# Causal attention with decay and a mixer: the 64-key tile transposed two query tiles at a time, its low part moved by DMA

## The chip, the cores and the metric

The kernel runs on one core of a Trainium2 chip. The metric is the device time of one execution in microseconds (us). PE is the matmul engine, DVE the vector engine, ACT the scalar engine, POOL is GpSimd, and SP issues the DMAs.

## The reference

For 8 batches and 8 heads, with 576 positions and head dimension 64, then a mixer over tokens and channels:

```python
scores = scale * np.matmul(q, k.transpose(0, 1, 3, 2))
cum = np.cumsum(np.log(np.clip(f, 0.0001, 1.0)), axis=-1)
decay = cum[:, :, :, None] - cum[:, :, None, :]
scores = np.where(causal, -1000000000.0, scores + decay)
attn = np.exp(scores - np.max(scores, axis=-1, keepdims=True))
attn = attn / (np.sum(attn, axis=-1, keepdims=True) + 1e-09)
x = np.matmul(attn, v)                    # heads side by side: 512 channels
h = np.maximum(x.T @ w_tok1, 0.0) @ w_tok2
u = x + h.T
out = u + np.maximum(u @ w_ch1, 0.0) @ w_ch2
```

## The kernel before, in words

The 576 positions are five tiles: tile 0 has 64, tiles 1 to 4 have 128. There are 64 heads, one after another, in an attention stage; the token mixer of each batch and part of the channel mixer run inside that stage, the rest of the channel mixer behind it (the channel stage). Numbers that need more than one pass of the fast matmul are split in a high part and a low part ("hi" and "lo"), and a product is made of three matmuls. The first four heads (`fv`) are done without parts.

For each head: PE makes the scores of each query tile against all earlier keys (L1031); DVE finds the minimum of the negated scores (L1038); ACT makes the exponentials into the tile `pr` (L1045), with the five query tiles side by side; DVE makes the reciprocals of the sums (L1063, L1066); POOL multiplies each query tile by them (L1073, five instructions). Then PE transposes `pr` block by block into PSUM (L1087): 15 blocks of query tile and key tile per head. For key tiles 1 to 4 ACT writes the high part to SBUF (L699) and DVE the low part (L708).

Key tile 0 has 64 keys, so its blocks give 64 rows. The block of query tile 0 is transposed in the group of key tile 2 (`t2`), the four others in the group `trs0`. Their high parts go to rows 0 to 63 of the tile `p0`, their low parts to the tile `low`, both in two pieces (64 and 512 columns). POOL then moves the low parts from `low` to rows 64 to 127 of `p0` (`hi_pool`, L702). One matmul over all 128 rows (L1159, L1160) then takes the high and low part at once. There is one buffer each of `p0` and `low`; L1159 is the first matmul of a head's output and reads `p0`, and the following head's `trs0` needs `p0` free.

The order on each engine is fixed before the launch: every operation gets a number for its place from the table `PR` (by kind of operation, `k0` to `k127`), and a planner goes through the engines in this order with its own costs and assigns buffers. Each engine, and SP as queue of the DMAs, works in this order and waits for what an instruction needs.

Of the kernel before, what the change touches and what calls it, by code (L numbers as in the profile page):

```python
# [15 lines left out]
P = 128  # L16
# [7 lines left out]
    k0=(0,),  # L24
    k1=(1, 0,),
# [17 lines left out]
    k20=(5, 16,),
    k21=(4, 10,),
    k22=(5, 10, 13, 19,),
    k23=(1, 0, 2, 4, 5, 3, 8, 6, 7, 21, 15, 18, 27, 25, 24, 36, 37, 35, 51, 53, 49, 56, 60, 52, 73, 75, 79, 91, 88, 87, 104, 105, 106, 114, 115, 116, 137, 135, 133, 145, 150, 147, 164, 167, 171, 179, 183, 185, 198, 202, 201, 213, 215, 217, 225, 230, 226, 240, 242, 241, 261, 263, 262, 275, 280, 279, 291, 293, 297, 308, 315, 310, 321, 327, 323, 343, 346, 341, 356, 357, 362, 373, 376, 375, 388, 394, 390, 405, 408, 406, 421, 425, 424, 437, 439, 438, 450, 452, 458, 464, 467, 472, 486, 491, 488, 503, 501, 500, 520, 523, 522, 534, 533, 536, 552, 554, 551, 564, 565, 568, 582, 589, 586, 601, 604, 606, 618, 621, 620, 633, 642, 637, 653, 656, 655, 673, 672, 669, 685, 690, 682, 699, 709, 703, 722, 718, 717, 735, 733, 737, 752, 754, 758, 763, 766, 769, 781, 787, 782, 796, 802, 801, 814, 816, 815, 832, 837, 834, 845, 863, 861, 857, 859, 872, 878, 891, 886, 894, 897, 906, 911, 923, 922, 929, 930, 937, 941, 946, 952, 955, 953, 959,),
    k24=(13, 10, 12, 14, 20, 29, 27, 31, 32, 33, 41, 30, 38, 34, 35, 56, 47, 49, 53, 55, 67, 61, 63, 60, 62, 76, 77, 79, 75, 78, 93, 95, 98, 92, 100, 101, 106, 108, 94, 97, 118, 119, 121, 123, 124, 139, 133, 137, 131, 134, 151, 153, 158, 152, 154, 160, 166, 168, 164, 167, 187, 186, 189, 183, 184, 195, 199, 202, 198, 200, 217, 219, 221, 224, 226, 232, 237, 238, 239, 241, 255, 257, 259, 256, 258, 267, 270, 272, 273, 275, 284, 288, 289, 285, 287, 299, 301, 303, 298, 300, 321, 323, 325, 322, 324, 333, 341, 343, 338, 340, 350, 352, 354, 359, 361, 370, 379, 380, 373, 376, 384, 391, 392, 385, 388, 405, 408, 409, 404, 406, 419, 421, 423, 427, 428, 438, 441, 443, 440, 442, 452, 460, 462, 456, 458, 476, 472, 474, 470, 473, 490, 492, 493, 491, 495, 505, 507, 509, 506, 508, 518, 520, 522, 526, 528, 543, 536, 538, 542, 544, 556, 561, 562, 558, 559, 576, 577, 579, 570, 573, 592, 594, 596, 593, 595, 608, 609, 611, 610, 614, 626, 631, 632, 627, 629, 645, 640, 643, 646, 649, 658, 667, 668, 662, 663, 675, 676, 678, 681, 683, 691, 694, 697, 693, 695, 709, 715, 717, 712, 714, 730, 732, 734, 733, 736, 752, 751, 753, 747, 749, 767, 771, 772, 760, 764, 781, 786, 787, 783, 784, 799, 794, 798, 793, 796, 811, 808, 809, 813, 814, 826, 827, 829, 831, 833, 837, 839, 842, 843, 845, 860, 861, 864, 856, 858, 870, 880, 881, 874, 878, 895, 889, 893, 888, 890, 904, 909, 911, 907, 908, 918, 932, 933, 929, 931, 934, 927, 928, 940, 945, 949, 960, 961, 955, 957, 962, 964, 967, 975, 976, 981, 990, 992, 987, 989, 994, 995, 997, 1006, 1007, 1017, 1016, 1021, 1020, 1022, 1028, 1024, 1025, 1031, 1034,),
# [610 lines left out]
def build(nc, env, dims):  # L658
# [296 lines left out]
    for n in range(HB):  # L955
# [139 lines left out]
        for g, kind, pb in (((3, 4), "t3", p34), ((2,), "t2", p2_), ((1,), "t1", p1_)):  # L1095
# [4 lines left out]
            def trs(ps=ps, blocks=blocks, w=w, first=g == (2,), tr=tr):  # L1100
# [965 lines left out]
```

## Time and profile before

| | us |
|---|---|
| median of 3 runs | 1017.48 (1015.66 to 1018.0) |
| the profiled execution | 1015.77 |
| its span | 1014.0 |
| PE busy in the span | 998.8 (99%) |
| DVE busy | 816.7 (81%) |
| ACT busy | 687.5 (68%) |
| POOL busy | 428.2 (42%) |

The span is the time from the first to the last instruction in the profile; the execution's own time lies 1.8 us above it. Matmuls are pipelined, so a PE that is busy all the time isn't a PE at its peak. POOL has next to nothing to do after the attention stage, so its share of the span says little about that stage.

### The profile page before, as it was taken

How to read it: one execution, taken by the hardware profiler on the slowest of the kernel's cores; microseconds unless marked ns; L12 is line 12 of the kernel's file. 1: busy time of each engine (PE TensorE's matmuls, PEld its weight loads, DVE VectorE, ACT ScalarE, POOL GpSimd, SP SyncE). 2: the span in 40 equal slices, each digit the busy share in tenths (PEclk: the TensorE clock that was granted, in tenths of full speed). 3: DMA queues.
4: the chain of work that ended last, by engine and by line, in shares of the span. 5: the costliest groups of instructions: out<-in, count | busy, mean ns of one | idle time of the engine just before them, and what ended most of it. 6: DMA issues, size and time to landing. Idle time of an engine off the chain costs nothing.

```text
span 1014.0 us, 19130 instructions
## 1 busy us (share of the span) xinstructions
PE 998.8 (99%) x6146; PEld 877.6 (87%) x6146; DVE 816.7 (81%) x1932; ACT 687.5 (68%) x1708; POOL 428.2 (42%) x530
## 2 busy tenths in 40 slices
PE   8999999999999999999999999999999999999998
PEld 5678899989999999999999988888888878888886
DVE  8899999898999897888885466879669756975695
ACT  7998899897888888878895533665266445543651
POOL 7688778878787886896862100000000000000000
PEclk9999999999999999999999999999999999999999
DMA  8865788876877765556426688727725762574054
GB/s 240 272 228 191 243 292 291 298 260 231 294 259 274 274 225 199 195 195 228 165 97 242 220 281 272 240 65 233 239 89 146 238 192 67 157 247 150 11 171 161
DMA packets 110595, 212.21 MB, mean 209 GB/s; under 512 B 13296, under 2 KB 51184, under 8 KB 109472
## 3 DMA queue, kind: packets, MB, share of 16 engines
q1 hardware_dynamic: 110496, 210.99, 62.4%
q8 instruction: 49, 0.80, 0.3%
q14 instruction: 50, 0.41, 0.1%
HBM read 113.26 MB, written 44.04 MB: 155 GB/s over the span
## 4 chain that ended last, share of the span: by engine, by line
PE 83%; DVE 8%; ACT 3%; issue 2%; DMA 2%; POOL 1%; SPq 0%; DVEq 0%; POOLq 0%; ACTq 0%
PE bank L1087 8%; PE bank L1576 6%; PE bank L1578 6%; PE bank L1577 6%; PE bank L1514 6%; PE bank L1516 6%; PE bank L1515 6%; PE bank L1031 5%; PE pair L1031 3%; PE pair L1169 3%; PE pair L1171 2%; ACT pr L1045 2%; PE bank L1686 2%; PE bank L1783 2%; PE bank L1687 2%
## 5 line engine op out<-in xcount | busy, mean ns | idle before, releaser
L1073 POOL TENSOR_SCALAR pr<-pr,rec 64x64 f32<-64x64 f32 (+4 forms) x320 | 171.6, 551 | 47.7 <-DVE rec L1066 18.2
L699 ACT ACTIVATE p<-bank 128x384 fp32r<-128x384 f32 (+3 forms) x300 | 130.4, 473 | 22.6 <-PE bank L1087 19.1
L1087 PE MATMUL bank<-ident,pr 128*128 128x128 f32 (+1 forms) x960 | 140.4, 274 | 4.7 <-DVE low L708 2.6
L1045 ACT ACTIVATE pr<-bank,nmin 64x64 f32<-64x64 f32 (+3 forms) x256 | 118.3, 471 | 12.5 <-DVE nmin L1038 10.4
L1087 PEld LDWEIGHTS bank<-ident,pr 128*128 128x128 f32 (+1 forms) x960 | 106.4, 131 | 21.6 <-DVE low L708 2.9
L708 DVE TENSOR_TENSOR p<-bank,p 128x384 fp32r<-128x384 f32 (+1 forms) x180 | 105.3, 590 | 10.6 <-ACT p L699 10.1
L1038 DVE CUSTOM_DVE_ANT_0 bank<-bank,mask 128x448 f32<-128x448 f32 (+3 forms) x256 | 106.5, 432 | 6.2 <-PE bank L1031 4.8
L1578 PE MATMUL bank<-ring,w2r 128*128 128x512 f32 x244 | 94.9, 389 | 0.0
L1031 PE MATMUL bank<-k 128*128 128x320 f32 (+1 forms) x480 | 83.3, 303 | 0.7 <-ACT pr L1045 0.6
L1576 PE MATMUL bank<-ring,w2r 128*128 128x512 f32 x212 | 82.5, 389 | 0.0
L1577 PE MATMUL bank<-ring,w2r 128*128 128x512 f32 x212 | 82.5, 389 | 0.0
L699 ACT ACTIVATE ring<-xt 128x512 fp32r<-128x512 f32 (+1 forms) x86 | 54.6, 649 | 35.8 <-DVE xt L1482 18.0
L1171 PE MATMUL pair<-p,vv 128*128 128x512 f32 x240 | 76.4, 321 | 0.0
L950 POOL TENSOR_TENSOR hl<-raw,hl 128x1152 fp32r<-128x1152 f32 x27 | 72.5, 2684 | 1.4
L1169 PE MATMUL pair<-p,vv 128*64 128x512 f32 x240 | 69.8, 332 | 0.0
L1031 PEld LDWEIGHTS bank<-k 128*128 128x128 f32 (+1 forms) x480 | 62.3, 176 | 3.3 <-ACT pr L1045 0.9
L699 ACT ACTIVATE ring<-h 128x512 fp32r<-128x512 f32 x63 | 38.3, 626 | 38.5 <-DVE h L1541 16.9
L708 DVE TENSOR_TENSOR low<-bank,p 64x512 fp32r<-64x512 f32 (+1 forms) x120 | 52.3, 442 | 10.8 <-ACT p L699 9.0
L699 ACT ACTIVATE ring<-bank 128x288 fp32r<-128x288 f32 (+2 forms) x96 | 47.1, 498 | 19.4 <-PE bank L1757 11.3
L702 POOL TENSOR_SCALAR p<-low 64x576 fp32r<-64x576 f32 x60 | 40.5, 676 | 40.2 <-DVE low L708 27.8
L705 POOL TENSOR_TENSOR ring<-xt,ring 128x576 fp32r<-128x576 f32 x32 | 45.9, 1442 | 25.4 <-ACT ring L699 25.1
L1045 ACT ACTIVATE pr<-pair,nmin 128x576 f32<-128x576 f32 x64 | 47.3, 739 | 10.2 <-DVE nmin L1038 7.1
(197 smaller groups left out, 3069.4 us busy)
## 6 DMA issues: line engine op xcount, KB each, us to landing
k<-hl SPq DMA_DIRECT2D x180, 288.0 KB
w2r<-sd SPq DMA_DIRECT2D x80, 256.0 KB
raw<-in_qk SPq DMA_DIRECT2D x60, 288.0 KB
w2r<-wd SPq DMA_DIRECT2D x60, 256.0 KB
vr<-in_v SPq DMA_DIRECT2D x32, 320.0 KB
ud<-xt SPq DMA_DIRECT2D x8, 1152.0 KB
pd<-part SPq DMA_DIRECT2D x32, 288.0 KB
dd<-in_w_ch SPq DMA_DIRECT2D x12, 512.0 KB
```

The source lines that it names most:

```text
L699: nc.scalar.activation(out, in_, func, scale=scale)
L708: nc.vector.tensor_tensor(out, in_, asf(hi), op=ALU.subtract)
L1031: nc.tensor.matmul(ps[:m, of : of + w], k[:, 0, i0 : i0 + m], k[:, 1, j0 : j0 + w], start=(x == 0), stop=(fq or x == 1))
L1038: nc.vector.tensor_tensor_reduce(x, x, E["mask"][:m, a : a + w], -1.0 / D**0.5, 3e38, op0=ALU.add, op1=ALU.min, accum_out=E["nmin"][sm][:m ...
L1045: nc.scalar.activation(at(pr)[:m, poff[t] : poff[t] + w], at(buf)[:m, of : of + w], AF.Exp, bias=E["nmin"][sm][:m, t : t + 1], scale=-1.0, ...
L1073: nc.gpsimd.tensor_scalar(x, x, r, 0.0, op0=ALU.mult, op1=ALU.add)
L1087: nc.tensor.transpose(out, at(pr)[:, poff[i] + start[j] : poff[i] + end[j]], E["ident"])
L1169: nc.tensor.matmul(x[:D], at(vv)[:, v0 + j, :D], at(pb)[:, 1, c0 : c0 + w], start=False, stop=last)
L1171: nc.tensor.matmul(x, at(vv)[:, v0 + j, :], at(pb)[:, 0, c0 : c0 + w], start=False, stop=last)
L1576: nc.tensor.matmul(o_, wh[:, ms], h_, start=first and pr == 0, stop=False, skip_group_check=not first)
L1577: nc.tensor.matmul(o_, wl[:, ms], h_, start=False, stop=False, skip_group_check=not first)
L1578: nc.tensor.matmul(o_, wh[:, ms], l_, start=False, stop=pr == PH - 1, skip_group_check=not first)
```

## The change

The five blocks of key tile 0 are no longer transposed one by one. Query tile 0 is transposed as a 64 x 64 block. Query tiles 1 and 3, and 2 and 4, go in pairs: POOL's normalisation writes the first 64 columns of query tile 1 to a place right ahead of query tile 3 (and those of 2 ahead of 4), for which `pr` has 64 columns more in two places, and one transpose of 128 columns turns both. The result has query tiles 1 and 2 in rows 0 to 63 and 3 and 4 in rows 64 to 127. So ACT writes high parts over all 128 rows in pieces of 320 and 256 columns, and DVE makes one low part of 128 x 320. Where the high part stands in rows 0 to 63 of `p0`, the low part is put in rows 64 to 127, and the other way round; two DMAs on SP move them there. The move by POOL is gone. Every number of the table `PR` is new. `hold`, a new field of the planner, and the costs changed with it bear on the planner's times alone.

```diff
-    poff = [sum(end[:t]) for t in range(NS)]
+    poff = [sum(end[:t]) + T0 * max(0, t - 2) for t in range(NS)]
+    MID = T0 + 2 * P
...
-        def norm(t, sm=sm, pr=pr):
...
+        def norm(t, a, z, to, sm=sm, pr=pr):
             m = size[t]
+            x, y = (at(pr)[:m, c : c + z - a] for c in (poff[t] + a, to))
+            nc.gpsimd.tensor_scalar(y, x, E["rec"][sm][:m, t // 2, t % 2 : t % 2 + 1], 0.0, op0=ALU.mult, op1=ALU.add)
...
         for t in (4, 3, 2, 1, 0):
+            a = T0 if t in (1, 2) else 0
+            p.op("POOL", d_pts(end[t] - a, 1), n + o["nrm"], lambda t=t, a=a, f=norm: f(t, a, end[t], poff[t] + a), rd=[("rec", sm)], wr=[(pr, t)], bufs=[pr])
+            if a:
+                p.op("POOL", d_pts(a, 1) + 50, n + o["nrm"], lambda t=t, a=a, f=norm: f(t, 0, a, poff[t + 2] - a), rd=[("rec", sm), (pr, t, "e")], wr=[(pr, t, "z")], bufs=[pr])
...
-                if first:
-                    tr(at(ps)[:T0, w : w + P], 0, 0)
...
-        def trs0(ps=ps, tr=tr):
-            for i in range(1, NS):
-                tr(at(ps)[:T0, (i - 1) * P : i * P], i, 0)
...
+        def trs0(ps=ps, pr=pr):
+            x, y = at(ps), at(pr)
+            nc.tensor.transpose(x[:, :T0], y[:T0, :P], E["ident"][:T0, :T0])
+            for z in (0, 1):
+                nc.tensor.transpose(x[:, T0 + z * P : T0 + (z + 1) * P], y[:, poff[z + 3] - T0 : poff[z + 3] + T0], E["ident"])
...
-            p.op("ACT", d_act(512), n + LAG + o["t0"] + o["hl"], lambda ps=ps, pb=p0_: hi_act(at(pb)[:T0, T0:], at(ps)[:T0, :]), rd=[ps], wr=[(p0_, "h1")], bufs=[ps, p0_])
+            p.op("ACT", d_act(MID), e0, lambda ps=ps, pb=p0_: hi_act(at(pb)[:, :MID], at(ps)[:, :MID]), rd=[ps], wr=[(p0_, 0)], bufs=[ps, p0_])
             p.op(
-                "DVE", d_dve(512), n + LAG + o["t0"] + o["hl"], lambda ps=ps, pb=p0_, lb=low: lo_dve(at(lb)[:, T0:], at(ps)[:T0, :], at(pb)[:T0, T0:]),
...
+                "DVE", d_dve(MID), e0, lambda ps=ps, pb=p0_, lb=low: lo_dve(at(lb), at(ps)[:, :MID], at(pb)[:, :MID]),
...
-            p.op(
-                "POOL", d_pts(S) + 110, n + LAG + o["t0"] + o["lo0"], lambda pb=p0_, lb=low: hi_pool(at(pb)[T0:, :], asf(at(lb))),
...
+            p.op("ACT", d_act(S - MID), e0, lambda ps=ps, pb=p0_: hi_act(at(pb)[:, MID:], at(ps)[:, T0:MID]), rd=[ps], wr=[(p0_, 1)], bufs=[ps, p0_])
+            dma(e0, lambda pb=p0_, lb=low: nc.sync.dma_start(asf(at(pb)[T0:, :MID]), asf(at(lb)[:T0])), 81920, dur=600, rd=[low], wr=[(p0_, 0)], bufs=[p0_, low])
+            dma(e0, lambda pb=p0_, lb=low: nc.sync.dma_start(asf(at(pb)[:T0, MID:]), asf(at(lb)[T0:, T0:])), 65536, dur=600, rd=[low], wr=[(p0_, 1)], bufs=[p0_, low])
...
-        ("pr", [P, 64 + 192 + 320 + 448 + 576], F32),
+        ("pr", [P, 64 + 192 + 320 + 64 + 448 + 64 + 576], F32),
...
-        ("low", [D, S], F32R),
+        ("low", [P, 64 + 256], F32R),
```

How the order moves is shown at two places. The numbers behind a name tell one buffer from another.

On PE in the middle of the attention stage, before the change: the transposes of one head (out of `pr_182`; the group of key tile 2 first, its fourth block is that of query tile 0; then key tile 1; then the four blocks of `trs0`), among output matmuls of the head ahead of it.

```order
L1087 MATMUL bank_65<-ident,pr_182 128x128 x3
L1087 MATMUL bank_65<-ident,pr_182 64x128
L1169 MATMUL pair_71<-p_189,vv_180 64x512
L1171 MATMUL pair_71<-p_189,vv_180 128x512
L1087 MATMUL bank_66<-ident,pr_182 128x128 x4
L1087 MATMUL bank_64<-ident,pr_182 64x128 x4
L1169 MATMUL pair_71<-p_188,vv_180 64x384
L1171 MATMUL pair_71<-p_188,vv_180 128x384
```

The same place with the change (line numbers are those of the changed kernel: L1119 and L1121 are `trs0`, L1088 the other blocks, L1156 and L1158 output matmuls, L1640 the mixer's transposes).

```order
L1119 MATMUL bank_64<-ident,pr_183 128x64
L1121 MATMUL bank_64<-ident,pr_183 128x128 x2
L1156 MATMUL pair_71<-p_189,vv_180 64x512
L1158 MATMUL pair_71<-p_189,vv_180 128x512
L1088 MATMUL bank_66<-ident,pr_183 128x128 x3
L1640 MATMUL bank_65<-ident,xt_151 128x128 x4
L1156 MATMUL pair_71<-p_187,vv_180 64x384
L1158 MATMUL pair_71<-p_187,vv_180 128x384
L1088 MATMUL bank_64<-ident,pr_183 128x128 x4
```

The tile's three transposes now stand ahead of the head's other groups, not behind them. From the row L1121 to the first matmul that reads this head's `p0` (L1146) follow 30 rows, with 15 transposes of 128 columns and matmuls of 7488 columns together.

On SP in the second half of the attention stage, before the change: k are the loads for the scores, raw those of q and k, dd, gd and ge weights on their way, ud the mixer's result.

```order
L964 DMA raw_172<-in_qk 64x1152
L1004 DMA k_176<-hl_175 64x1152
L1004 DMA k_178<-hl_175 64x2x576
L1004 DMA k_177<-hl_175 64x1152
L1004 DMA k_176<-hl_175 64x2x576
L1004 DMA k_177<-hl_175 64x2x576
L1004 DMA k_179<-hl_175 64x2x576
```

With the change, at the same place:

```order
L1137 DMA p_190<-low_191 64x256
L1136 DMA p_190<-low_191 64x320
L1722 DMA ud_130<-xt_150 128x2304
L910 DMA gd_116<-dd 128x1024
L1001 DMA k_178<-cc_192 2x1x576
L1007 DMA k_176<-hl_175 64x1152
L1137 DMA p_190<-low_191 64x256
L1136 DMA p_190<-low_191 64x320
L790 DMA dd<-in_w_ch 128x256
L967 DMA raw_172<-in_qk 64x1152 x2
L1007 DMA k_176<-hl_175 64x2x576
```

The two DMAs of each head's low part (L1136, L1137) stand between the loads, as pairs, and the loads of later heads stand behind them.

## Rows read from the trace of the kernel before

**Rows 1.** The page: busy time, share of the span and instructions of each engine.

```profile
PE 998.8 (99%) x6146; PEld 877.6 (87%) x6146; DVE 816.7 (81%) x1932; ACT 687.5 (68%) x1708; POOL 428.2 (42%) x530
```

**Rows 2.** Busy time by stretches: window, length, engines' busy us, clock, DMA share, GB/s.

```profile
60.00:541.00 481.00, 474.10 (x3662) 449.92 (x3661) 427.24 (x1225) 412.30 (x1139) 380.56 (x458) 1.00 0.66 232
541.00:1014.00 473.00, 467.58 (x2171) 390.96 (x2169) 338.38 (x548) 224.29 (x424) 5.75 (x4) 1.00 0.57 180
700.00:800.00 100.00, 100.00 (x443) 82.77 (x441) 78.12 (x119) 50.09 (x90) 0.00 (x0) 1.00 0.60 184
...
```

**Rows 3.** The chain that ended last: shares of the span by engine, by line.

```profile
PE 83%; DVE 8%; ACT 3%; issue 2%; DMA 2%; POOL 1%; SPq 0%; DVEq 0%; POOLq 0%; ACTq 0%
...
by line: PE bank L1087 8.1%; PE bank L1576 6.0%; PE bank L1578 6.0%; PE bank L1577 6.0%; PE bank L1514 6.0%; PE bank L1516 6.0%; PE bank L1515 5.9%; PE bank L1031 5.3%; PE pair L1031 2.6%; PE pair L1169 2.5%; PE pair L1171 2.5%; issue 2.3%;
```

**Rows 4.** Timeline of one head, 345 to 351 us: start, duration, instruction.

```profile
344.98 0.60 PE L1087 MATMUL bank<-ident,pr 128*64 128x128 f32 x4
...
345.68 0.60 ACT L699 ACTIVATE p<-bank 64x512 fp32r<-64x512 f32 x1
...
346.38 0.68 DVE L708 TENSOR_TENSOR low<-bank,p 64x512 fp32r<-64x512 f32 x1
...
347.88 0.19 DVE L708 TENSOR_TENSOR low<-bank,p 64x64 fp32r<-64x64 f32 x1
...
348.65 0.67 POOL L702 TENSOR_SCALAR p<-low 64x576 fp32r<-64x576 f32 x1
...
348.89 0.49 PE L1087 MATMUL bank<-ident,pr 128*128 128x128 f32 x3
...
351.07 0.39 PE L1159 MATMUL pair<-p,vv 128*128 128x512 f32 x1
```

**Rows 5.** Groups by line, whole span: count, busy us, mean ns, idle before.

```profile
L1087 PE MATMUL bank<-ident,pr 128*128 128x128 f32 (+1 forms) x960 | 140.4, 274 | 4.7 <-DVE low L708 2.6 <-DVE xt L1724 1.4 <-DVE rec L1066 0.2
```

**Rows 6.** Groups by line and shape, DVE, ACT and POOL, 60 to 541 us.

```profile
L708 DVE TENSOR_TENSOR low<-bank,p 64x512 fp32r<-64x512 f32 x59 | 39.9, 676 | 7.0 <-ACT p L699 6.2 <-issue 0.3
L708 DVE TENSOR_TENSOR low<-bank,p 64x64 fp32r<-64x64 f32 x59 | 12.2, 207 | 3.8 <-ACT p L699 2.8 <-issue 0.6
...
L699 ACT ACTIVATE p<-bank 64x512 fp32r<-64x512 f32 x59 | 34.7, 589 | 2.9 <-PE bank L1087 2.3
L699 ACT ACTIVATE p<-bank 64x64 fp32r<-64x64 f32 x59 | 12.5, 212 | 2.4 <-PE bank L1087 2.2
...
L702 POOL TENSOR_SCALAR p<-low 64x576 fp32r<-64x576 f32 x59 | 39.9, 676 | 40.1 <-DVE low L708 27.8 <-PE pair L1171 3.4 <-ACT xt L1209 2.5
L1073 POOL TENSOR_SCALAR pr<-pr,rec 128x320 f32<-128x320 f32 x58 | 31.0, 536 | 5.1 <-ACT p L699 4.4
L1073 POOL TENSOR_SCALAR pr<-pr,rec 128x192 f32<-128x192 f32 x58 | 25.3, 437 | 6.4 <-DVE rec L1066 2.8 <-ACT p L699 2.6 <-PE bank L1087 0.5
L1073 POOL TENSOR_SCALAR pr<-pr,rec 64x64 f32<-64x64 f32 x57 | 19.1, 337 | 7.0 <-PE pair L1031 3.5 <-ACT xt L1209 1.6 <-DVE rec L1066 1.1
```

**Rows 7.** DMA issues on SP, lines L998 and L1004: min/median/max ns.

```profile
L998 SPq DMA_DIRECT2D k<-cc x120: 557/632/1397, 26.6 to 515.8; - x120
...
L1004 SPq DMA_DIRECT2D k<-hl x180: 465/624/1516, 16.3 to 514.6; - x180
```

**Rows 8.** DMA issues in 60 to 541 us: transfer, count, KB each.

```profile
k<-hl SPq DMA_DIRECT2D x163, 288.0 KB
...
dd<-gd SPq DMA_DIRECT2D x4, 256.0 KB
```

**Rows 9.** Timeline, two DMAs and the instructions that waited for them.

```profile
465.48 0.54 SPq L964 DMA_DIRECT2D raw<-in_qk  x1
...
468.90 1.16 POOL L942 TENSOR_SCALAR hl<-raw 128x1152 fp32r<-128x1152 f32 x1 [0.57 <-DMA raw<-in_qk]
...
497.05 0.54 SPq L973 DMA_DIRECT2D vr<-in_v  x1
...
501.40 0.74 ACT L940 ACTIVATE vv<-vr 128x640 fp32r<-128x640 f32 x1 [0.72 <-DMA vr<-in_v]
```

More of the change, by code (lines that the diff above doesn't have):

```diff
@@ L23 @@
 PR = dict(
-    k0=(0,),
-    k1=(1, 0,),
+    k0=(1,),
+    k1=(0, 1,),
     k2=(0,),
@@ L498 @@
 class Op:
-    __slots__ = ("eng", "dur", "head", "tail", "lat", "fn", "prio", "bufs", "need", "outs", "ready", "start", "idx", "port", "grp")
+    __slots__ = ("eng", "dur", "head", "tail", "lat", "fn", "prio", "bufs", "need", "outs", "ready", "start", "idx", "port", "grp", "hold")
 class Plan:
@@ L528, in op @@
         o.head = o.tail = 0.0
+        o.hold = hold
         if eng == "PE":
@@ L561, in run @@
         engine_at = dict.fromkeys(queue, 0.0)
+        held = dict.fromkeys(queue, False)
         unit, nexts, fifo = {}, {}, {}
@@ L640, in run @@
                 done = end + o.lat
-            engine_at[e] = end
+            engine_at[e], held[e] = end, o.hold[1]
             if o.port:
@@ L1113, in build @@
                 continue
-            two = [(p0_, "h0")] if g == (2,) else []
             p.op("ACT", d_act(w), n + LAG + o[kind] + o["hl"], lambda ps=ps, pb=pb, w=w: hi_act(at(pb)[:, 0, :], at(ps)[:, :w]), rd=[ps], wr=[(pb, 0)], bufs=[ps, pb])
-            if two:
-                p.op(
-                    "ACT", d_act(T0), n + LAG + o[kind] + o["hl"], lambda ps=ps, w=w, pb=p0_: hi_act(at(pb)[:T0, :T0], at(ps)[:T0, w : w + T0]),
-                    rd=[ps], wr=two, bufs=[ps, p0_],
-                )
@@ L1121, in build @@
             p.op(
                 "DVE", d_dve(w), n + LAG + o[kind] + o["hl"], lambda ps=ps, pb=pb, w=w: lo_dve(at(pb)[:, 1, :], at(ps)[:, :w], at(pb)[:, 0, :]),
-                rd=[ps, (pb, 0), *two], wr=[(pb, 1)], bufs=[ps, pb],
+                rd=[ps, (pb, 0)], wr=[(pb, 1)], bufs=[ps, pb],
             )
-            if two:
-                p.op(
-                    "DVE", d_dve(T0), n + LAG + o[kind] + o["hl"],
-                    lambda ps=ps, w=w, pb=p0_, lb=low: lo_dve(at(lb)[:, :T0], at(ps)[:T0, w : w + T0], at(pb)[:T0, :T0]),
-                    rd=[ps, (pb, 0), *two], wr=[(low, 0)], bufs=[ps, p0_, low],
-                )
@@ L1200, in build @@
             p.op(
-                "ACT", d_act(S) + 130, fo,
+                "ACT", d_act(S), fo,
                 lambda av=av, half=half, xt=xt, h=h: nc.scalar.activation(at(xt)[half, h // 2, :], at(av)[:D, off : off + S], AF.Copy),
-                rd=[(av, 0)], wr=[(xt, h)], bufs=[av, xt],
+                rd=[(av, 0)], wr=[(xt, h)], bufs=[av, xt], hold=(h % 2, h % 2),
             )
@@ L1208, in build @@
             p.op(
-                "ACT", d_act(S) + 130, fo, lambda av=av, xt=xt, half=half, other=other, h=h: nc.scalar.activation(at(xt)[half, h // 2, :], at(av)[other, off : off + S], AF.Copy),
-                rd=[(av, 0)], wr=[(xt, h)], bufs=[av, xt],
+                "ACT", d_act(S), fo, lambda av=av, xt=xt, half=half, other=other, h=h: nc.scalar.activation(at(xt)[half, h // 2, :], at(av)[other, off : off + S], AF.Copy),
+                rd=[(av, 0)], wr=[(xt, h)], bufs=[av, xt], hold=(1, 1),
             )
```

287 lines of the change are left out of this document (137 added, 150 removed).

## The prediction

> **What bounds the kernel now.** I read the busy times first. Over the span PE is busy 99% and no other engine above 81% [rows 1]. By stretches, the attention stage (60 to 541 us) and the channel stage behind it (541 to 1014 us) differ [rows 2]. In the channel stage PE works almost alone: 443 matmuls of 512 columns in 100 us, 226 ns each, without a gap. In the attention stage four engines are nearly full: PE 474.1 of 481 us, DVE 427.2 (89%), ACT 412.3 (86%), POOL 380.6 (79%). The clock granted is 1.00 in both, the higher level of 2.4 GHz. A busy PE is not PE at its peak, so I went to the chain of waits for what a saved PE instruction is worth [rows 3]. Of the chain 83% is PE and 8% DVE; the attention transposes (L1087) hold 8.1% of the span, 82.1 us. The timeline of one head gives their spacing [rows 4]: four take 0.60 us and three 0.49 us, so one more costs 0.11 us whether 64 or 128 columns are loaded. The 960 of them [rows 5] are thus 960 x 0.109 = 105 us of PE work, and 82.1/105 = 78% of it sets the end. The rest lies where another engine is late.
>
> **The change part by part.** *PE.* Per head, 15 transposes of 128 columns become 12 of 128 and one of 64. The 64-column one is in no trace; it moves half the columns, so I take 55 ns, with the bounds 0 and 109 ns. Removed: 2.5 x 0.109 = 0.27 us per head, 17.5 us over 64 heads. If the shortened ones stand on the chain as often as the others, 82.1 x 2.5/15 = 13.7 us goes from the end. The bounds are 10.9 us (the small one costs a whole transpose: 82.1 x 2/15) and 17.5 us (all of it stands on the chain).
>
> *DVE.* The two pieces of the low part take 676 and 207 ns [rows 6]: 1.047 ns per column and 140 ns. One piece of 320 columns is then 475 ns, 408 ns less per head; 24.5 us over the 60 heads that have low parts. Eight per cent of the chain is DVE, so most of this is slack. Pro rata of the stage (8% of 1014 us is 81 us, out of 817 us of DVE work, 10%) it is worth 2.5 us; bounds 0 and 24.5.
>
> *ACT.* The pieces of 512 and 64 columns (589 + 212 ns) become pieces of 320 and 256, by the same line 427 + 374 ns: the same 801 ns. Nothing.
>
> *POOL.* The move of the low part goes, 676 ns. Two normalisations are split: 437 ns becomes 387 + 337, and 536 ns becomes 487 + 337 (by the slope between 192 and 320 columns, and 337 ns for 64), so 575 ns comes. Net 0.1 us less per head, at 79% busy: nothing. The memsets that fall away at the start lie under the first transfers: nothing.
>
> *SP and the DMAs.* In place of the POOL move, two DMAs per head are issued on SP, 80 and 64 KB. Issues of this kind hold SP 0.62 to 0.63 us each [rows 7], and 451 were issued in the stage (the sum of thirteen counts, of which [rows 8] shows the first and the last): 284 of 481 us. With 117 more, 358 us, 74%. SP issues in order, so what stands behind a low part's DMA that waits for DVE is the loads of k and raw for later heads, as the order shows. PE waits for none of those loads in the list of waits that I read, so they have time in hand; I take nothing, and up to 3 us as the other bound.
>
> *The new wait.* The first matmul on p0 now waits for a landing, not for POOL. In the head of [rows 4] ACT starts 0.10 us after the transposes end, DVE 0.10 us after ACT ends, POOL ends at 349.32 us, and the matmul starts at 351.07 us, 1.75 us later: the chain is covered. Now, from the last transpose's spacing on: 0.16 (its remaining time, 0.27 - 0.11) + 0.10 + 0.43 (ACT) + 0.10 + 0.48 (DVE) + 0.10 + 0.62 (the first DMA's issue, ahead of the second) = 1.99 us, and the landing of the second. The trace has no DMA of 64 to 80 KB that something waited for. The nearest rows [rows 9]: 288 KB issued at 465.48 us released POOL at 468.90, 3.42 us; 320 KB took 4.35 us, with others in the queue. At the stage's mean of 232 GB/s 288 KB are 1.27 us and 80 KB 0.35 us, so about 3.42 - 1.27 + 0.35 = 2.5 us; bounds 2.15 us (no time for the bytes at all) and 4.35 us. Against this stands the PE work that the new order has between the tile's last transpose and the first matmul on p0. I added it for each head (0.441 ns per column, 226/512, and 0.109 us per transpose): in the head shown with the change 15 transposes and 7488 columns, 4.9 us; over the 60 heads least 4.0, median 5.6 us. With a landing of 2.5 us the chain is 4.5 us, longer than the cover in under a dozen heads, by 2 us in all. With scatter around it I take 3 us; bounds 0 and, at 4.35 us, about 55 us.
>
> On such transfers the Trainium skill speaks against the change: DMA: Bandwidth & Descriptors, section "Rules for kernel authors", says that under 64 KB one pays mostly overhead, and advises one 128-partition transfer instead of two to disjoint halves, which serialize. Its section "Anatomy of one DMA — SWDGE (gpsimd) path" gives about 2.0 us and bytes/436e3, from another issuing path; for 80 KB that is an estimate of 2.2 us, by which this wait would be nearly 0 and the sum 3 us better. No row here shows it; my 2.5 us stays.
>
> *The channel stage.* The order is new there too, but its instructions are the same. PE is idle 473 - 467.6 = 5.4 us in it, so no more than that can be won; I take 0 with bounds of -5 and +3 us.
>
> **Sum.** -13.7 - 2.5 + 3 = -13.2 us against the profiled execution's 1015.8 us (span 1014.0 and 1.8 us around it): 1002.6 us. That execution was 1.7 us below the median of 1017.5 us, inside the scatter of the three runs, so I forecast 1002.5 us for the changed kernel's median.
>
> **The rivals.**
> *More than the sum.* All 17.5 us of PE work comes off the end, because DVE, relieved by 408 ns per head, no longer makes PE wait, and part of DVE's 24.5 us comes off besides. For it: DVE's 89% is the next highest, and it holds 81 us of the chain. Against it: ACT at 86% is not relieved at all. Price: 17.5 us alone gives 998; with 3 to 10 us of DVE's 985 to 996. Chance 0.20.
>
> *The landing takes the place of the POOL move, and the kernel is slower.* The place is the first matmul on p0 in each head. With the cover as counted, a chain of 5.3 us (a mean landing of 3.3 us) costs 16 us over the 60 heads and eats the whole gain; beyond that each further 0.2 us costs some 6 us. For it: 288 KB landed in 3.42 us, DMA engines are busy 66% of the stage, p0 has one buffer, so a late head delays its successor's transposes too. Against it: 80 KB are a quarter of the bytes, and PE's work between takes longer than my count, since PE waits elsewhere too. At 3.3 us it gives 1015 to 1017, at 3.6 us (25 us by the cover as counted, where my sum has 3) 1024. Chance 0.10 for slower, 0.05 for no change, and 0.10 that it eats part and leaves 1008 to 1013.
>
> *The change does not do what it says:* the transposes saved lie where PE waits for DVE or ACT. Then the 22% off the chain would be nearer to all. The share of L1087 on the chain speaks against it; it is inside the no-change case.
>
> **How the numbers follow.** My forecast (996 to 1008 us) has 0.55, the better case 0.20, the partly eaten one 0.10, no change 0.05, slower 0.10. Leaving out the lower half of the better case and what is above the partly eaten one's upper end, the range is 990 to 1012 us. About 0.2%, 2 us, is what a measurement can tell from no change: faster 0.85, same 0.05, slower 0.10.
>
> **What would show it.** Right: 832 rows of attention transposes, 0.33 us or less for the tile's three; low on DVE near 475 ns; no POOL move; attention ending 10 to 16 us earlier with the same share of PE idle; the channel stage within 5 us of 473. The landing step is wrong if PE waits for a DMA p<-low in sum over 5 us, or if a landing takes over 3 us. The SP step is wrong if PE or POOL wait for k or raw. The forecast fails if DVE or ACT hold more of the chain than before, or if the channel stage moves by more than the 5 us.

## The result, and the profile after

The changed kernel takes 1026.45 us in the median (1025.2 to 1029.4), the kernel before 1017.61 us beside it: ratio 1.0095, 95% interval 1.007 to 1.012. It is 9 us slower, where 15 us less were forecast. The profiled execution took 1029.4 us (span 1027.6).

The page's busy times, which answer to [rows 1]:

```profile
PE 1005.3 (98%) x6019; PEld 870.1 (85%) x6019; DVE 805.9 (78%) x1869; ACT 691.4 (67%) x1708; POOL 420.7 (41%) x598
```

By stretches (columns as in [rows 2]):

```profile
60.00:541.00 481.00, 470.71 (x3466) 433.24 (x3467) 407.56 (x1158) 407.96 (x1125) 367.05 (x508) 0.99 0.74 249
541.00:1027.00 486.00, 481.18 (x2275) 403.74 (x2273) 348.40 (x566) 235.79 (x452) 11.37 (x15) 1.00 0.56 179
```

PE, DVE, ACT and POOL are all less busy in the attention stage than before: something holds them together. The last attention transpose starts at 557.9 us (before 539.6), and from there to the end it takes 469.8 us (before 474.4). So all of the loss lies in the attention stage (its last 17 us stand in the second row). The chain that ended last, which answers to [rows 3], from the page:

```profile
PE 85%; DMA 5%; DVE 4%; ACT 2%; issue 2%; SPq 1%; ACTq 0%; DVEq 0%
PE bank L1501 6%; PE bank L1503 6%; PE bank L1563 6%; PE bank L1502 6%; PE bank L1564 6%; PE bank L1565 6%; PE bank L1088 6%; PE bank L1034 5%; DMA p<-low 4%; PE pair L1156 3%; PE pair L1158 3%; PE pair L1034 2%; PE bank L1121 2%; PE pair L1146 2%; PE bank L1673 2%; PE bank L1674 2%
```

DVE fell from 8 to 4% of it, POOL is gone, and the DMA of the low part has come in with 4%. But PE itself holds more of it than before, with 128 transposes fewer. Two places show why.

**The tile's transposes.** The timeline of PE, and of its weight loads (PEld), where a head's tile 0 follows other transposes:

```profile
348.11 0.60 PE L1088 MATMUL bank<-ident,pr 128*128 128x128 f32 x4
348.64 0.27 PE L1119 MATMUL bank<-ident,pr 64*128 64x64 f32 x1
348.84 0.44 PE L1121 MATMUL bank<-ident,pr 128*128 128x128 f32 x2
349.04 0.42 PE L1156 MATMUL pair<-p,vv 128*64 128x384 f32 x1
```

```profile
348.01 0.46 PEld L1088 LDWEIGHTS bank<-ident,pr 128*128 128x128 f32 x4
348.64 0.13 PEld L1119 LDWEIGHTS bank<-ident,pr 64*128 64x128 f32 x1 [0.17 <-issue]
348.84 0.20 PEld L1121 LDWEIGHTS bank<-ident,pr 128*128 128x128 f32 x2
349.01 0.14 PEld L1156 LDWEIGHTS pair<-p,vv 128*64 128x64 f32 x1
```

Four transposes take 4 x 0.109 = 0.44 us to the next start, but the 64-row one (L1119) starts 0.53 us after the first: 0.09 us late. The next one starts 0.20 us behind it, not 0.11, and L1156 0.20 us behind that, where one transpose (0.11) and the step to a matmul (0.03) make 0.14. The loads say what happens: those of the four run ahead (348.01 to 348.47 for matmuls from 348.11), but the load of 64 rows starts only with its own matmul, at 348.64, and the next load of 128 rows at 348.84, also with its matmul. Between 64 and 128 rows a load no longer runs ahead of the matmul in front of it. Over the 64 heads the two intervals are 203 and 165 ns in the median.

The trace of the kernel before has the same. In the first four heads its output matmuls L1159 and L1160 load 64 rows among instructions that load 128:

```profile
22.62 0.66 PE L1087 MATMUL bank<-ident,pr 128*128 128x128 f32 x4
23.20 1.07 PE L1159 MATMUL pair<-part,vr 64*64 64x512 f32 x2
24.11 0.27 PE L1160 MATMUL pair<-part,vr 64*64 64x64 f32 x2
24.32 0.55 PE L1087 MATMUL bank<-ident,pr 128*128 128x128 f32 x3
```

By the single records L1159 starts 0.20 us after the last transpose (one transpose starts 0.11 us after another), and the next transpose starts 0.15 us after the second L1160, which started 0.055 us after the first: 0.09 us lost each way. The other three heads have the like. It is the rows: L1159 and L1160 load 64 columns where the transposes load 128, but one L1160 (at 52.05 us) is followed by L1167, 128 rows and 64 columns too, and there as well it is 0.15 us. And a matmul that moves 64 columns on 128 rows (L1147) loses nothing: in e1 below, where the small transpose has 128 rows, that one starts 0.03 us after it. From 97 rows (L1031) to 128 nothing is lost: at 26.39 us the load of a transpose behind it starts 0.37 us before its own matmul.

**The low part's way.** One head, ACT and DVE, then SP's queue, then PE (a number in brackets is idle time before, and what ended it):

```profile
231.73 0.27 PE L1119 MATMUL bank<-ident,pr 64*128 64x64 f32 x1
...
232.40 1.76 ACT L702 ACTIVATE p<-bank 128x320 fp32r<-128x320 f32 x4
...
232.87 0.49 DVE L711 TENSOR_TENSOR low<-bank,p 128x320 fp32r<-128x320 f32 x1
...
232.24 0.64 SPq L1001 DMA_DIRECT2D k<-cc  x1
232.93 0.72 SPq L790 DMA_DIRECT2D dd<-in_w_ch  x1
233.76 1.09 SPq L976 DMA_DIRECT2D vr<-in_v  x2
234.95 0.52 SPq L1137 DMA_DIRECT2D p<-low  x1
235.56 0.55 SPq L1136 DMA_DIRECT2D p<-low  x1
...
239.54 0.47 PE L1146 MATMUL pair<-p,vv 128*128 128x512 f32 x1 [1.63 <-DMA p<-low]
```

DVE is done at 233.36, but SP is in the middle of other issues and takes the first of the two DMAs 1.6 us later, the second 2.2 us later; it lands 3.9 us after its issue, and PE has stood for 1.63 us. From the records of all 60 heads: SP's first issue comes 0.03 us after DVE in the median but 0.29 in the mean; a landing takes 2.33 us in the median, and 40 of 120 take over 3 us (1.9 to 4.6). The group of the first matmul on p0 (whole span; busy us, mean ns, idle before):

```profile
L1146 PE MATMUL pair<-p,vv 128*128 128x512 f32 x60 | 26.5, 442 | 6.6 <-DMA p<-low 6.3 <-DVE xt L1711 0.2
```

and in 60 to 541 us, among the waits (us in total, times, longest):

```profile
POOL hl L945 <- DMA k<-hl: 13.0, 7, 3.6
```

The loads of k are late too. Before, and in the run e6 below, which has the new order without these DMAs, it was

```profile
POOL hl L942 <- DMA k<-hl: 2.0, 2, 1.8
```

```profile
POOL hl L945 <- DMA k<-hl: 9.9, 5, 4.6
```

so most of this wait stands in the new order without the DMAs, and some 3 us came with them.

### The profile page after: what moved, and what is told of

The parts are those of the page before. It is cut to its first block, busy times and chain, and to the rows that moved or that the text cites. A ratio compares the mean times of both kernels' runs of the same rounds, so it can differ in the third digit from the quotient of the medians.

```text
span 1027.6 us, 19093 instructions
## 1 busy us (share of the span) xinstructions
PE 1005.3 (98%) x6019; PEld 870.1 (85%) x6019; DVE 805.9 (78%) x1869; ACT 691.4 (67%) x1708; POOL 420.7 (41%) x598
## 4 chain that ended last, share of the span: by engine, by line
PE 85%; DMA 5%; DVE 4%; ACT 2%; issue 2%; SPq 1%; ACTq 0%; DVEq 0%
PE bank L1501 6%; PE bank L1503 6%; PE bank L1563 6%; PE bank L1502 6%; PE bank L1564 6%; PE bank L1565 6%; PE bank L1088 6%; PE bank L1034 5%; DMA p<-low 4%; PE pair L1156 3%; PE pair L1158 3%; PE pair L1034 2%; PE bank L1121 2%; PE pair L1146 2%; PE bank L1673 2%; PE bank L1674 2%
## 5 line engine op out<-in xcount | busy, mean ns | idle before, releaser
L1074 POOL TENSOR_SCALAR pr<-pr,rec 128x64 f32<-128x64 f32 (+5 forms) x448 | 207.1, 480 | 75.6 <-DVE rec L1069 45.5
L702 ACT ACTIVATE p<-bank 128x384 fp32r<-128x384 f32 (+3 forms) x300 | 133.8, 480 | 38.1 <-PE bank L1088 15.5
L1048 ACT ACTIVATE pr<-bank,nmin 128x448 f32<-128x448 f32 (+3 forms) x256 | 118.3, 468 | 13.0 <-DVE nmin L1041 11.3
L1088 PE MATMUL bank<-ident,pr 128*128 128x128 f32 x640 | 98.8, 275 | 2.7 <-DVE p L711 0.6
L1088 PEld LDWEIGHTS bank<-ident,pr 128*128 128x128 f32 x640 | 75.5, 141 | 14.8 <-issue 2.1
L1158 PE MATMUL pair<-p,vv 128*128 128x512 f32 x240 | 76.8, 323 | 0.0
L1156 PE MATMUL pair<-p,vv 128*64 128x512 f32 x240 | 72.1, 341 | 0.0
L702 ACT ACTIVATE ring<-bank 128x512 fp32r<-128x512 f32 (+2 forms) x96 | 47.1, 497 | 19.2 <-PE bank L1674 7.3
L1501 PE MATMUL bank<-ring,w1r 128*128 128x512 f32 x145 | 56.4, 389 | 0.0
L1502 PE MATMUL bank<-ring,w1r 128*128 128x512 f32 x145 | 56.4, 389 | 0.0
L1565 PEld LDWEIGHTS bank<-ring,w2r 128*128 128x128 f32 x238 | 44.7, 188 | 9.3
```

What stands on the lines that cost most here:

```text
L702: nc.scalar.activation(out, in_, func, scale=scale)
L1048: nc.scalar.activation(at(pr)[:m, poff[t] : poff[t] + w], at(buf)[:m, of : of + w], AF.Exp, bias=E["nmin"][sm][:m, t : t + 1], scale=-1.0, ...
L1074: nc.gpsimd.tensor_scalar(y, x, E["rec"][sm][:m, t // 2, t % 2 : t % 2 + 1], 0.0, op0=ALU.mult, op1=ALU.add)
L1088: nc.tensor.transpose(out, at(pr)[:, poff[i] + start[j] : poff[i] + end[j]], E["ident"])
L1158: nc.tensor.matmul(x, at(vv)[:, v0 + j, :], at(pb)[:, 0, c0 : c0 + w], start=False, stop=last)
L1501: nc.tensor.matmul(q, wh[:, cs], h_, start=first and c == 0, stop=False, skip_group_check=not first)
```

## The experiments

All ratios are to the kernel before on the same chip, with 95% intervals. It took 1013.8 to 1017.4 us on these chips; expectations in us count from 1017.6.

One thing changes along with some edits. Where the planner foresees PE idle for more than 0.7 us, the kernel puts short fillers there (matmuls that load 16 columns, L773 before, L775 to L778 in the others). From 60 us on the kernel before has 21 of them, the changed one, e1, e2, e6 and e12 have 23, e4 21 and e10 16. Runs in which the planner's times moved have more: e18 67, e3, e5 and e11 106 to 126, e15 218, e16 476, e17 512, e13 844, e14 1020, e7 to e9 over 1500. In those, part of a wait shows as work of PE, and a filler that stands where PE would not have waited is a cost of its own.

**128 rows, and no DMAs, one at a time.** Theory A: the 64-row transpose; B: the landing; C: the new order. The edit of e1 (the lower rows of that block are zeroed once at the start, as before), and of e2:

```diff
-            nc.tensor.transpose(x[:, :T0], y[:T0, :P], E["ident"][:T0, :T0])
+            nc.tensor.transpose(x[:, :P], y[:, :P], E["ident"])
```

```diff
-            dma(e0, ... asf(at(pb)[T0:, :MID]), asf(at(lb)[:T0]) ...)
-            dma(e0, ... asf(at(pb)[:T0, MID:]), asf(at(lb)[T0:, T0:]) ...)
```

e1: 

> The changed kernel with the small transpose loading all 128 rows (its lower rows zeroed once) where it loads 64; its surplus columns are overwritten by the next transpose. Theory A (the 64-row transpose costs PE a gap before it and two behind it: 94 + 94 + 56 ns against a 128-row one, read from the changed kernel's trace): the tile's three transposes go from 0.48 to 0.33 us, the gap ahead shrinks too, 64 x 0.244 = 15.6 us of PE work, so 1010 to 1015 us. Theory B (the landing of the two DMAs of the low part is the whole loss): 1024 to 1028 us, since nothing of the DMAs changes. Theory C (the new order is the loss): 1024 to 1028 us as well.

e2: 

> The changed kernel without the two DMAs, so the low part of tile 0 is not delivered and the first matmul on p0 waits for ACT alone. Theory A: only the wait at that matmul goes, 9.9 us by the gaps of the trace, so 1014 to 1019 us. Theory B: at least the 24 us between forecast and result go, 1003 us or less. Theory C: 1022 to 1027 us.

Measured: e1 1.0049 (1.003 to 1.0068), e2 1.0050 (1.003 to 1.0071). Each gives back 4.6 us of the 9.7. In the expectations' terms they are 1022.6 and 1022.7 us. e1 lies where no theory had it: more gain than B and C allow, less than A said. e2 lies between A and B on the one side and the changed kernel on the other, at the lower end of C's range. In e1 the tile runs as A says:

```profile
345.13 0.49 PE L1088 MATMUL bank<-ident,pr 128*128 128x128 f32 x3
345.45 0.27 PE L1119 MATMUL bank<-ident,pr 128*128 128x128 f32 x1
345.56 0.38 PE L1121 MATMUL bank<-ident,pr 128*128 128x128 f32 x2
345.70 0.42 PE L1156 MATMUL pair<-p,vv 128*64 128x384 f32 x1
```

0.32, 0.11 and 0.14 us: the gaps are gone, 0.09 + 0.09 + 0.06 = 0.24 us per head, 15 us in all. But the time fell by a third of that, and the first matmul on p0 waited longer:

```profile
L1146 PE MATMUL pair<-p,vv 128*128 128x512 f32 x60 | 26.4, 440 | 10.4 <-DMA p<-low 8.3 <-DVE nmin L1041 1.4 <-DVE xt L1711 0.6
```

**The 64-row transpose alone, in the kernel before.**

```diff
-                    tr(at(ps)[:T0, w : w + P], 0, 0)
+                    nc.tensor.transpose(at(ps)[:T0, w : w + T0], at(pr)[:T0, :T0], E["ident"][:T0, :T0])
```

> The kernel before with one edit: the one transpose of tile 0 with itself loads 64 rows (64x64) where it loaded 128. Order, POOL move and all else stay. Theory A: 64 x 0.244 = 15.6 us more PE work, 78 to 100% of it at the end: 1028 to 1034 us. Theories B and C: no change or up to 3 us faster, 1014 to 1018 us, since the transpose has half the columns to move.

Measured 1.0119 (1.0097 to 1.0141), 12 us slower, for a transpose with half the columns and half the rows; 0.78 x 15.6 us is 12.2. PE's timeline of that run:

```profile
343.43 0.49 PE L1087 MATMUL bank<-ident,pr 128*128 128x128 f32 x3
343.85 0.24 PE L1104 MATMUL bank<-ident,pr 64*64 64x64 f32 x1
344.02 0.63 PE L1087 MATMUL bank<-ident,pr 128*64 128x128 f32 x4
344.40 0.42 PE L1169 MATMUL pair<-p,vv 128*64 128x384 f32 x1
```

L1104 starts 0.42 us after the three began (0.33 without a gap), the next 0.17 us later, and the four behind it take 0.63 where [rows 4] has 0.60. Theory A's price holds in a kernel that has nothing else of the change.

**Both at once.**

> Both edits at once, in the new order: the small transpose on 128 rows, and the two DMAs of the low part left out (the low part of tile 0 is not delivered). The two edits alone gave 0.46 and 0.45 per cent. If the 64-row gaps and the landing wait are separate costs, the sum: ratio to before 1.000. If the one hid the other (with 128 rows alone the wait for the landing grew from 9.9 to 14.5 us), the 14.5 us go as well: 1.0049 - 0.0143 = 0.991 to 0.995, near the 14 us of PE work that the change really takes out. If the new order is the loss (theory C), it stays above 1.000.

Measured 0.9911 (0.9879 to 0.9944): 9 us faster than before, the second of the three outcomes; with that theory C, the new order as the loss, is out. So from the fastest upward: without DMAs the 64 rows cost 1.39% (0.9911 to 1.0050), 14 us; with 128 rows the DMAs cost 1.38%, 14 us; whichever comes second costs 4.6 us. By the intervals each of these is known to 3 or 4 us. The costs hide each other: gaps on PE in front of the matmul on p0 are cover for the landing. Of the 9 us hidden, 3.8 are seen as such, the idle time before that matmul, which grew from 6.6 to 10.4 us; the way of the rest isn't shown.

**What the DMAs cost: the wait or the load.** The same DMAs, written to a tile that nobody reads:

```diff
-asf(at(pb)[T0:, :MID])   wr=[(p0_, 0)], bufs=[p0_, low]
+asf(E["spare0"][T0:, :MID])   wr=["sp0"], bufs=[low]
```

> The new order, the small transpose on 128 rows, both DMAs at their places in SP's queue with their bytes, but written into a spare tile that nothing reads, so the first matmul on p0 waits for ACT alone (the low part of tile 0 is not delivered). If the wait is the cost: as without the DMAs, ratio 0.989 to 0.995. If the load on SP's queue and the DMA engines is the cost: as with them, 1.002 to 1.007. Half and half: 0.996 to 1.000.

Measured 0.9971 (0.9948 to 0.9994): 0.6% (6 us, against e6) is load, 0.8% (8 us, against e1) is the wait, each known to 3 or 4 us. In e12's waits of SP's queue and of POOL:

```profile
SPq L1136 <- DVE low L711: 14.6, 7, 4.0
...
SPq L1137 <- DVE p L711: 9.4, 6, 5.0
```

```profile
POOL hl L945 <- DMA k<-hl: 12.0, 5, 4.6
```

SP stands at L1136 until DVE has the low part, and the loads of k wait behind it. But POOL's wait for them is 2 us longer than e6's 9.9, not 6. PE, which in e6 waits for no load, waits for loads of k in e12:

```profile
PE bank L1034 <- DMA k<-cc: 1.2, 2, 0.8
...
PE pair L1034 <- DMA k<-hl: 0.6, 1, 0.6
```

How all of the 6 us come about, and whether by SP's queue or by the traffic of the DMA engines, isn't shown.

**The DMAs' place in SP's queue.** Of the table only the two DMAs' ranks move, in the kernel with 128 rows, and the fillers with them (in e14 the planner places the DMAs when it has the low part ready; 0 to 15 places later, 3.1 in the mean):

```diff
-    k64, k65: rank of each DMA
+    k64, k65: rank - 1.5   (e15)    rank - 2.5   (e16)    rank + 2.5   (e17)
```

e14: 

> As the run with 128 rows alone (1.0049), but the two DMAs are put into SP's queue where the planner has the low part ready, not at their old ranks. DVE's end to the first issue took 0.62 us in the median there and up to 2.7 us; if the delay in SP's queue feeds the wait, 0.998 to 1.002; if it is the landing (2.3 to 4.6 us) alone, 1.003 to 1.007.

e15: 

> 128 rows, new order, the first of a head's two DMAs a place earlier in SP's queue or none (mean 0.6). If the place was late by the planner's fault: 0.999 to 1.003 against 1.0049 with the old places. If SP then waits for the low part and holds up the loads behind it: 1.005 to 1.012.

e16: 

> The same with one to two places earlier (mean 1.5). If late places are a part of the loss: 0.995 to 1.001; if SP's wait for the low part takes it back: above 1.006.

e17: 

> The same with one to two places later (mean 1.5), each place being an issue of 0.5 to 0.6 us. If the whole delay comes out at the end, 60 x 0.8 = 50 us: 1.05; by the 9 per cent of 2.9 places, 1.045. If only the heads count that wait already (23 of 60), 23 x 0.8 = 18 us: 1.02.

Measured against e1's 1.0049: e15 1.0333 (1.0305 to 1.0361), e16 1.0634 (1.0615 to 1.0654), e17 1.0534 (1.0501 to 1.0567), e14 1.0934 (1.0898 to 1.097). e15 and e14 lie far above all that was expected of them. The place was not late: with the fillers that each place brings, both directions lose. One place or two later costs 4.8%, 49 us; 0.8 us per head for 1.5 places of 0.54 us, the whole delay, would make the same, as e17's first bound had it. One place of e17:

```profile
101.04 1.27 PE L776 MATMUL pair<-lower 128*16 128x128 f32 x19
104.49 0.47 PE L1146 MATMUL pair<-p,vv 128*128 128x512 f32 x1 [2.18 <-DMA p<-low]
```

Of the 41 us by which e17's profiled span is longer than e1's, 27 lie under fillers and 9 are idle time of PE. After 17 of the 31 stretches of fillers PE still waits, so there the wait is real; after the other 14 (13 us) it doesn't, and there the filler may be the cost. In e15, 13 of 19 stretches (11 us of the 27 lost) have no wait behind them, in e16 24 of 33 (22 of 57). So what a place alone costs is not shown. Earlier loses by another way; e16's waits of SP's queue and of POOL:

```profile
SPq L1136 <- DVE low L711: 32.4, 13, 5.6
SPq L1137 <- DVE low L711: 19.4, 6, 7.8
```

```profile
POOL hl L945 <- DMA k<-hl: 30.2, 9, 7.9
POOL hl L945 <- DMA p<-low: 11.0, 3, 6.1
```

SP now stands for the low part (the first row is 15.5 us in e1), and POOL for what stands behind it (the third is 13.3 us in e1).

**More cover for the landing.** Two p0 buffers, 128 rows, and p0's matmuls as the last of the head's accumulation:

```diff
-nc.tensor.matmul(x[:, 512:1024], w_, r_[:, T0:], start=True, stop=False)   (first)
+nc.tensor.matmul(x[:, 512:1024], w_, r_[:, T0:], start=fv, stop=not fv)    (last, 60 heads)
```

> A correct version that keeps both DMAs: the small transpose on 128 rows, two p0 buffers, and in each of the 60 heads the matmuls on p0 moved behind the other ten of their accumulation (the first of these now starts it), so PE has more work between the transposes of tile 0 and the first matmul on p0: 2560 columns by 226/512 ns, 1.1 us, and what the order puts between. If the two costs found (64-row gaps, landing beyond the cover) are the whole loss, this comes near the run without DMAs and with 128 rows: ratio 0.990 to 0.996. If the DMAs also cost by what they hold up in SP's queue or on the DMA engines, 0.997 to 1.003. If the landings are late by more than 1.1 us in many heads, above 1.003.

Measured 1.0065 (1.0047 to 1.0082), the third outcome by its number but not by its reason: PE no longer waits at p0, yet nothing is won. The waits of that run in 60 to 541 us have in the wait's stead:

```profile
POOL hl L945 <- DMA k<-hl: 15.0, 5, 6.1
...
ACT xt L1201 <- PE pair L1147: 9.9, 12, 2.0
```

the late loads of k, as in e1 (13.3 us), and the output's copy, which now waits for p0's matmuls (in e1 for L1158, 5.6 us). Since the output and the copy moved with the matmuls, this run does not price the wait alone; e12 does.

**POOL in place of the DMAs.** Two copies `hi_pool(at(pb)[T0:, :MID], asf(at(lb)[:T0]))` and `hi_pool(at(pb)[:T0, MID:], asf(at(lb)[T0:, T0:]))`, placed where the planner has them ready; with 64 rows (e3), 128 rows (e5), and e10's matmuls last (e11).

e3: 

> The changed kernel with two POOL copies (64x320 and 64x256) in place of the two DMAs, taken up by POOL when they are ready by the planner's times; all else as changed. POOL gets some 0.8 us per head, 50 us. Theory A: the wait for the landing goes, a part comes back as waits for POOL, 1015 to 1024 us. Theory B: 1005 us or less. Theory C: 1022 to 1030 us.

e5: 

> The new order, the small transpose on 128 rows, two POOL copies in place of the DMAs. With 64 rows this had 1.0169. If the two costs behave as with the DMAs, the 128 rows give 0.5 to 1.4 per cent back: 1.003 to 1.012. If POOL is the bound of that run, nothing comes back: 1.014 to 1.019.

e11: 

> As e10 (128 rows, two p0 buffers, p0's matmuls last), with two POOL copies in place of the DMAs. It shows whether the copy by DMA is any better than by POOL once there is cover: if POOL's 0.8 us per head are hidden, as e10 within 0.3 per cent; if POOL (82 to 90 per cent busy) is the bound, 1 per cent or more above e10.

Measured 1.0169 (1.0143 to 1.0195), 1.0103 (1.0082 to 1.0124), 1.0151 (1.0132 to 1.0171). e3 lies above all three theories, e5 in its first range, e11 near its second outcome. 128 rows again give 0.66% back. The copies are no better than the DMAs, but that they are worse isn't shown: e5 is 5.5 us above e1, and 5.2 us more of its span lie under fillers.

**DVE writing straight across.** DVE subtracts twice (64x320, 64x256) and writes each piece to p0's other half, with no low tile and no transport:

```diff
-lo_dve(at(lb), at(ps)[:, :MID], at(pb)[:, :MID])
+lo_dve(at(pb)[T0:, :MID], at(ps)[:T0, :MID], at(pb)[:T0, :MID])
+lo_dve(at(pb)[:T0, MID:], at(ps)[T0:, T0:MID], at(pb)[T0:, MID:])
```

> New order, the small transpose on 128 rows, no DMAs and no low tile: DVE subtracts twice, 64x320 and 64x256, and writes each piece straight to the other half of p0's partitions (the second one stands behind the next DVE instruction). DVE gets some 0.4 us per head more than in the changed kernel, 24 us, at 85 per cent busy. If the transport is the rest of the loss, near the run without DMAs and with 128 rows (0.9911): 0.990 to 0.997, faster than before. If DVE's added work makes PE wait by its share of the chain, 1.000 to 1.006; if DVE becomes the bound, above 1.006.

Measured 1.0354 (1.0331 to 1.0376). The second piece takes 0.43 us, 26 us of DVE's time, and the run is 45 us above e6, so it costs more than its time (3 us more than in e6 lie under fillers). PE's longest wait and the page's chain:

```profile
PE bank L1087 <- DVE p L710: 6.8, 11, 1.4
```

```profile
PE 70%; DVE 14%; ACT 9%; issue 4%; DMA 2%; POOL 1%; SPq 0%; ACTq 0%; DVEq 0%; POOLq 0%
```

PE's waits for DVE's pieces (L710) sum to 13.6 us in four rows, where e6 has 2.1 us, and DVE holds 14% of the chain. DVE has no slack at that place in this order. None of the complete versions beats the kernel before; e1 comes nearest.

**The order.** The change in the order of before (e7), with 128 rows (e8), and POOL (e9); and e13, the new order with tile 0's chain placed by the planner.

e7: 

> The change itself (64-row transpose, two DMAs), but every instruction in the order of the kernel before as far as it existed there; the split normalisations stand behind the piece that they are cut from, and the DMAs go to SP when the planner has them ready. Theory C (the new order costs time of its own): faster than the changed kernel, ratio 1.000 to 1.006. Theories A and B: 1.007 to 1.016, the 64-row gaps and the landing wait come along, and the old order was not made for a landing behind the low part.

e8: 

> As the one before it, in the old order, with the small transpose on 128 rows. Theory A: 0.4 to 1.2 per cent less than that one. Theory C: also below 1.0049, the ratio of the same edit in the new order; else above it.

e9: 

> The old order, the small transpose on 128 rows, and two POOL copies in place of the DMAs. It keeps what the change saves on PE (14 us of work) and DVE and drops the landing; POOL gets 0.6 to 0.7 us more per head than before. Theories A and B: 0.985 to 0.997. If POOL becomes the bound, as it may in the run with POOL copies in the new order (1.0169): above 1.005.

e13: 

> A correct version: 128 rows, two p0 buffers, and the whole chain of tile 0 (transposes, ACT, DVE, ACT, DMAs) placed by the planner as early as its inputs and buffers are ready, with the first matmul on p0 where it was. If cover is what is missing, the wait at that matmul falls under 4 us and the ratio is 0.991 to 0.999; if the earlier transposes only wait for POOL's normalisations instead, 1.000 to 1.010.

Measured 1.147, 1.1449, 1.1275 and 1.0793 (intervals of 0.4% or less to either side). e7, e9 and e13 lie far above all that was expected of them, and e8 above the theories A and C; in e13 PE stands 24.1 us for p<-low at the matmul on p0, where cover would have left under 4. All four let the planner place the new steps, and e14 shows 9% from that on SP's queue alone, fillers included. They do not tell what the new order costs against the old one.

## Why the prediction was wrong

**The step that failed first: "The 64-column one is in no trace; it moves half the columns, so I take 55 ns, with the bounds 0 and 109 ns."** It was priced by its columns. The block itself is in no trace, but its kind is: the matmuls L1159 and L1160 of the first four heads, shown above, load 64 rows among 128 in the kernel before and lose 0.09 us each way. The small transpose also loads 64 rows among instructions that load 128, and that costs a gap ahead of it and two behind: 0.09 + 0.20 + 0.06 = 0.35 us per head with its own time, more than three times the upper bound. The rest of the step was right: three transposes fewer per head are 192 x 0.109 = 21 us of PE work. But the small one takes 64 x 0.35 = 23 us, so 2 us are lost where 17.5 us were to be won, 13.7 of them on the chain. e4 shows this without the rest of the change (12 us), e2 against e6 inside it (14 us). The old kernel's 64-key block was transposed on 128 rows, the lower ones zero; the memsets that fell away, counted at nothing, were what made that possible.

The Trainium skill had the rule: TensorEngine Tiling (Array Packing), section "Key Properties", says that a change of tiling mode, not just of tile, drains the engine. The traces here agree, with 0.09 us going in and 0.15 us coming out against a 128-row one; that the array drains is not itself in a trace.

**The new wait: mis-sized.** Taken at 3 us; 8 us by e12 against e1. The landing was right in the median (2.33 us, 2.5 taken; 2.7 in the mean). What was wrong is what stands around it. In the means of 60 heads ACT starts 0.28 us after the transposes end, DVE 0.32 us after ACT, and SP takes 0.29 us to come to the first DMA, where 0.10 was taken from one head for each; the second DMA follows 0.82 us behind the first, where an issue of 0.62 was taken. From the last transpose's spacing to the later landing it is 5.5 us in the mean, not 4.5, and the spread decides: of the 11 waits for p<-low 10 lie in heads whose second landing takes 3 us or more. The rival with the landing had the place and the mechanism: it put 16 us on a chain of 5.3 us. With 128 rows (e1) the chain is 5.6 us in the mean, for which the prediction's count of cover would give over 25 us; PE's time between, 6.1 us in the median where 5.6 were counted, leaves a wait of 8 us, and the DMAs cost 14 in all. So the DMAs alone turn a gain of 9 us into a loss of 5, at landings of 2.8 us in the mean, not the 3.3 us from which that rival counted.

**SP: mis-sized.** Taken at 0, with 3 us as the other bound; 6 us by e12 against e6. "PE waits for none of those loads" was true of the kernel before; with the DMAs in the queue PE waits for loads of k (1.8 us in e12, 0 in e6) and POOL for 2 us more of them. That is less than the 6 us, and POOL does not appear in the page's chain above, so the way of the rest stays open.

**Right:** the removed transposes (832 are left); DVE's low piece (489 ns in 60 to 541 us, 475 forecast); SP's issues (0.54 us, 0.62 forecast); the split normalisations (363 to 481 ns, 337 to 487 forecast); the channel stage within 5 us. DVE's 2.5 us can't be told apart: e6, with neither cost, stands at -9 us, where PE's 14 x 0.78 = 10.9 us and DVE's 2.5 would make -13.4 (e6's interval: -6 to -12). Of the 4 us that are missing, a fall of the clock has 1.7 in the profiled execution, as follows; the rest, and whether the new order holds it, stays open.

**Not in the sum: the clock.** Windows of the changed kernel (PE, PEld, DVE, ACT, POOL, clock):

```profile
50.00:60.00 10.00, 7.97 (x41) 4.63 (x40) 9.72 (x23) 7.01 (x20) 5.72 (x8) 1.00 0.62 215
60.00:70.00 10.00, 9.89 (x65) 8.80 (x66) 8.09 (x23) 8.56 (x23) 7.44 (x10) 0.83 0.59 190
230.00:240.00 10.00, 8.36 (x64) 7.29 (x62) 8.37 (x22) 8.13 (x24) 7.74 (x9) 1.00 0.92 321
240.00:250.00 10.00, 10.00 (x66) 9.31 (x65) 7.39 (x22) 7.22 (x22) 8.43 (x15) 0.83 0.62 215
```

After two stretches in which PE stood (the second ends with the 1.63 us shown above) the granted clock fell for a while from 2.4 to 1.2 GHz; 0.83 in the mean of 10 us is 1.7 us of work lost each time, 3.4 us in all. Before, it was 1.00 there. The first of the two does not come from the DMAs or the 64 rows, for e6 has it too:

```profile
60.00:70.00 10.00, 10.00 (x69) 9.23 (x68) 7.94 (x21) 8.68 (x25) 7.92 (x10) 0.83 0.58 200
```

Here PE was 81% busy in the 10 us ahead of it, before the change 98%. So a wait on PE can cost its own length once more, but most did not: e1 has 12 waits for p<-low and two such falls in the attention stage.

## What to carry to other kernels

Price a PE instruction by what it changes against its neighbours, not by its size, and look for the same change of neighbours elsewhere in the trace at hand: a 64-row operand among 128-row ones cost 0.24 us more than the full one, and zeroed rows are cheaper. When a transport goes to a queue that works in order, count three things: its own landing with its spread, the place where its turn comes, and who waits for what it holds up. And take two suspected costs away together as well as one at a time: here each alone gave 4.6 us and both 18.7.

## What was not expected of the hardware

A weight load of 64 rows takes as long as one of 128 rows (0.135 against 0.140 us in the median), but does not run ahead of a 128-row matmul, nor a 128-row load ahead of a 64-row one; the load after it is also late, by 0.06 us. A load of 128 rows behind a matmul of 97 does run ahead. Landings of 64 and 80 KB range from 1.9 to 4.6 us in the same stage. In this order of instructions a shift of two DMAs by one place or two in SP's queue, in either direction, costs 3 to 6%, the fillers that come with it included.
